# A written-out order of 2440 operations replaced by another: windowed attention and a token-mixing MLP, twice, on one core

## The chip, the cores and the metric

One of the eight cores of a Trainium2 chip runs the whole program. The metric is device time in microseconds, from the first to the last thing that the program does. The engines are PE (TensorE, matmuls; PEld is its weight load), DVE (VectorE), ACT (ScalarE), POOL (GpSimd) and SP (SyncE, which here issues all DMAs, in its own order).

## The reference

The input x has 2048 rows of 512 in bf16. Two layers of two parts each are applied, with the same weights in both layers:

```python
x = x + attention(layernorm(x), wqkv, wo)            # 32 heads of 16, row i sees rows i-255..i
x = x + mlp(layernorm(x), w1, b1, w2, b2)            # mixes the rows, not the columns:
#   h = layernorm(x);  u = gelu(h^T @ w1 + b1)       # 512 x 1792
#   y = (u @ w2 + b2)^T                              # 2048 x 512
```

The attention is `softmax(q k^T / 4 + window mask) v`, then a projection by `wo`. The LayerNorms have no gains, and the MLP's input is normalised twice.

## The kernel before, in words

x stays in SBUF as 16 tiles of 128 rows. Per layer the kernel goes through these steps.

- **LayerNorm** (`ln_blocks`, L499): statistics on DVE (L492, L494), the power -0.5 on POOL (L505), the normalised row tile `xh_sb` on DVE (L512). The two normalisations in a row before the MLP are done as one.
- **Transposed x and projections** (`qkv`, L556): four blocks of 512 rows. `xh_sb` is transposed on PE (L570, copied out at L577 by DVE or L579 by ACT) in the first block, and by DMA elsewhere (L563). PE then projects q, k and v in steps of two matmuls of 128x512 (all of these, and every other dense matmul, go through `mm_group`, L540, and so have line L534). The results leave PSUM by DVE or ACT: q at L592 or L594, k at L603 or L602, or through `stg` (L614) and then a masked copy on POOL or DVE (L629), or eight small DMAs on SP (L624), v at L649 or L651 and from there by DMA into `vb` (L654).
- **Attention** (`attention`, L682): 152 score steps in all, 76 a layer. A score step has 8 to 28 matmuls on quarter-height tiles (L710; L721 adds a mask bias in some steps of the first chunks), writes four of the eight PSUM banks, and is followed by two exponentials on ACT (L736), one for each pair of banks. Where the mask isn't added on PE, POOL multiplies part of the probabilities by zero or one (L757). A P·V step has 32 to 64 small matmuls (L774); two such steps fill two banks, which DVE transposes (L794), inverts (L798), and, after a product on POOL or DVE (L800 or the same line), transposes back into `oT` (L805).
- **Output projection** (`wo_block`, L810): PE by L534, then an addition on DVE (L816), and the LayerNorm for the MLP.
- **MLP**: `u_part` (L869) computes partial sums over the rows that are ready while the attention goes on, and parks them in SBUF (L880, L882, L884); `u_last` (L888, matmuls L895) adds the last rows, DVE adds the parked part (L906), ACT applies gelu (L910). `y_block` (L928) computes y with matmuls by L534 and adds it to x on DVE (L936); in layer 0 the next layer's LayerNorms and projections are mixed in. For the last row tile `y_last` (L914) does the same in two halves of 256 columns (L922). In layer 1 the rows are then written out (L982, halves L925).
- **Weights of the MLP** come tile by tile from HBM, 128 KB a DMA, into four buffers for w1 (`load_w1`, L825), and into two buffers for w2 and, for the first three pairs of row tiles, into free buffers of the probabilities (`load_w2`, L840). A load waits until the last reader of its place is done, and since SP issues in order, everything behind it on SP waits too.

**What sets the order.** None of these functions emits an instruction. Each calls `op` of `Graph` (L107), which records an operation with what it reads and writes; some operations carry alternatives on another engine (`alts`). At the end `Graph.replay` (L175) goes through a list of pairs (which of the operations left, which alternative), takes buffers in that order (`Pool.take`, L63), and appends each operation to its engine's queue; `Graph.emit` (L196) then writes five instruction streams, with semaphore waits for what an operation reads and for the earlier users of its buffers. The list is a constant: `ORDER` (L15), packed text, which `begin_order` (L44) unpacks:

```python
raw = zlib.decompress(base64.b85decode("".join(ORDER)))
left, out = list(range(n)), []
for lo, hi in zip(raw[:n], raw[n:]):
    k, alt = divmod(lo + 256 * hi, 4)
    out.append((left.pop(k), alt))
```

So the order on every engine, the engine of each movable operation, and which buffer a tile gets, are all in that text.

Of the kernel before, what the change touches and what calls it, by code (L numbers as in the profile page):

```python
# [11 lines left out]
P = 128  # L12


ORDER = (  # L15
    'c-p;IA&l$T6@5<LtlqS5E3foc@=E@aw=!@gw{j(~WMJTxyp>ln2uP~{Z)K250RaI90R{mEUMV0TAi%&NARr*XARr(hARr)MfI&b&KvV^!(trU0z0PDZG'
    'yl)uzq{)8{y&cW{N8={o_p?j=Ia9EYe}!&L?lJXYD57>h99@89fUDLp4X6kUl)BtcN|Bvzq7yl24gnw>EBc;?T`h*e!p}DhuPnGE8AYJ>?NDc-EU{JnQ'
    'J?<nJLSPGG|{)lB7yQMUn<-s^rO^wmT_FllgSHMyo7)=X^gB#doRt=XP6FyItG%ZO?`+R26o09>x<(6iusP_r={V77bOCO-)l(#u(3gZN@4UCbX31K~Y'
    'YpHNRo}@kqenZGLz6@UYz)#yfp|x8T?7wXO>bO%SFNVItfMN6Pd2j$$dw=3p3G-2P&<Y=g}gb4}CuEaQ3KR}^J1i1i*=oI^m0jRpykB*?Pc5`=D#Qkrx'
    'kzUzmb(QTUTJuml~KQvpz;jkIhr$Jx`RI0aYLEzVtR?wHE?mso@FZD*F(R5v1g*<O-UX8#F{M2gO?QUDEZE}IE8FM@zHW~>6t5j=MjnGaE0V$RhT9nXk'  # L20
    'w`-V&VR_!x6GdIuD-|+xMbF=7WV>}-*Cn@r1DLLlM&uo(13?r;ScW=0>-0J#jvpv*nNdV1lL^n-`_H#@x7lotBtPCC<2c?Q_J@^ux3R2^Y38Q0PWSu$z'
    'qdPQV4CI%Kmk-I<1r*VG^eu^wlvLdk`B|9F@=f!fgtoDu+K(Gk_2rL3ry+ts4NJOej|)Jov_ge^1N}Uv;sxJg;lFHr&fjfGRrs|7}GSY+~qlyWqG+eMX'
    '_GBbbUHC3@po1Ivz_<?P|5^7p40uf(rnoS&ce#-Fn+zg{EnthG7&Ak?vL;86i#t7qAr|Bgw!|G0P;GW*CDvwgH}sqSWo`Xe{tNY};%$Wu;!1Wr_$91c5'
    '^ga^e|P7|-}@f*2Ht@>SOr1bXm0l*d@6r_%{s7Yhh%O}GtsqPznIpleOwm&<Iym_S*Yf|DxiLEX38eR6|ibT%#(@6t3yBd`=o=ZBP`F1!G*3?qt~jYP4'
    'kgt)RULyJiWqa>-zYnVdn7<s;fTnJdD$Z{(Xu;Chp;~Fl)dZH(TfvsyQa_WYupjy*|*K)0fR8<2`nt?hN5Tu%UIz_`_C5@s%y#uV_J3$Z(0&Lrr3P!}R'
    'N4Bi5okqQ0Z%Fc9SF2k6Un;oJG=-AMVllVAow6MnO#9$&EWQIcTCLWXj5QiRemRN&0^uvxG6QJ2dZR8$;Hb_sCd+8IlPjoNMHQa^f}eho*+5MD*0Kn2D'
    'XCN{EnQb(vg>ve57%lAkN`Wji?L;UI*5j7Xoju;eeey``u-l@Km}w09XEKtPvKS(@Amt}av|YD?;y8ioF>U4fk62VA90;dM^<EwwlG#y#mi29)sN$}dH'
    'he*+v^7K!uK^?m;HbIy&$e6N0JkU4~}CTpyRf?{qA&{O_y0VnqW4}*=D;L4gq16VmzH<oK5X4gG8XkXX8m`nt}kKCgSgI?a_ENf_fq}91V}?2m#~WZim'
    'CLANG0<@TqH>F@P6wb&R=|>tafAvmF#V0|w3INEOM1U(>ejA!q5J6u<$u;sTsVqpEG++YUV(_KxdpWZ>7_vaETnHl02^)E0zz9-7VMnj(X8D@BtSh5@}'
    'F>6YCNLstdYElFUkNl_sEP;`i@_`YgX6jfr9^ZnoQd@{+$o2~EP<^CFbfa+{E1zD9mk4=HYUkd(c2r}XU!4t?6_K^52$tF5zDyZ+|gia^e_1)ocjG`z>'  # L30
    '@-*>0j~^sFZ`*ON(+ZFUUV|3QhgxaJqwh0j8?DwFl-jawWLw}K5C(;dpcRp6nU?LGPNs!TKm(ou;;%`8i@rb$&6cFYfldV2)f5R)fQJeYrQh!>P&7$yQ'
    'fm9YEAoOMY9Jx%{lh&JY6x6SQzHG5tgrw~fD>e%g<&|If~=0m(ReWIC(zj_jan@TEog%Vn=Qzlv_nEL4`9Yl6k1iw4PD0p7usKmsu!kqI!#hQBQ=V`aw'
    '2rd351J*zA*HF5Y$&Y96_fw4GxjbMpemru~v*_R9%1+wkD>!P}TV?QI&452OB3TA&^lIw88HXo)rCvJx6n#*wV1)_dQiL;3QIUo@0cmD9gH%0W*2F90?'
    '*C7AFb_5n*w3x{XQ5aYqQ$q9Bh56l&;zkfY*>5|ZacV6_mVX58=jy(NlKG>GEy#0G(Kp=X0ut5&UsehZ^EvVtaRG#i#v#kK?TRkbX>@M@TrYT1#BR7nM'
    ';!$ejrCPD*?Vl3)uYViW9uT}z#RCPG}RZjw486rN<^*e#bD@aA4bdG1D7>0PYI2^M5@^BbGOeQllo{WQ>F<SH$%kSZM1ZsqFFP_LyKY*&Af&kN0KJ*PE'
    '3?u3{+x~n$M`(!`i{_+g<~oKZu2wQQj0TM~brQoik!iG>aLBs`)Z8!tHIo`xLb5DM5IOp}_W4_bpMCV<**K1a3;JcoT^4ZXmE742hsx#i*bP_wme1oi*'
    'DcOtW$wBYei|yQ7$}u~YR4k_#|bwVub+sp1paPbq<HiAP`dmPL`wJ^#nS{*y2QYt3nb^fN>_03`IGlL|7vCQ_CvY+VOZt2f#hCzyxv^~xtAl5RjIfXae'
    'd4ni4uCl?N1e%d)}GDPa}^oaKDrs*Erq+;NvlWlmMkSAbX1L0?{*tAL-0}!0>B^k4w%Fa$Na?$*;QN?cU%%3gB;SfB1FFKEHC0!j-;+mA;1g{Qvi;^aA'
    'qIxhlow=KXp+*6XowuR!F^tl?gh_z6?YJyzj58*{H||Ev#>-B~W*UfSt(qurt><tP{b&bKgj_EWwLl;3YjRQ?GHmP({_&bNf#7Nk<?b?#4~6_?VJc3ep'
    'IDSaxwC(n9v{;=e(gZMQH_!*D#HJh7q!CiC#;L`&Bh{Xr(SjKOO#``JbYduOY^DmWN-EgIgdOX#={HYU!<31Frw+F5*{6fusMISs<@}&>%g@#-;g?s<~'  # L40
    'OMQHNd>npS#c|KeUZ(aUo&TXiaL>W~Tn+jtA%8<PdrLX5U|tT`r%#AiHF@vn=LPuxP~iUpKz>0O'
)

def begin_order(n):  # L44
# [971 lines left out]
```

## Time and profile before

| | |
|---|---|
| runs before | 446.86, 447.12 and 448.62 us, median 447.12 |
| profiled execution, span from first to last instruction | 443.6 us |
| what lies around the span | 3.3 to 5.0 us, by these runs (the profiled execution's own total is not listed apart) |
| PE busy | 426.4 us, 96%, 6344 matmuls |
| ACT busy | 317.4 us, 72% |
| DVE busy | 308.7 us, 70% |
| POOL busy | 207.9 us, 47% |
| granted TensorE clock | 1.00 throughout |
| DMA | 45.01 MB, mean 101 GB/s |

The profile is of one execution. Its lines name engine, source line, tiles and shapes; a line of a helper (L534) stands for many uses, told apart by their tiles. A "step" below is one recorded operation, for instance two matmuls of a projection. The stages in time: projections of the first blocks and first scores until some 57 us, attention of layer 0 with projections and partial MLP sums between until 151 us, the first MLP and the next layer's first projections until 215 us, attention of layer 1 until 360 us, the last MLP until the end.

### The profile page before, as it was taken

To read this page: it belongs to the slowest core of one execution; us is meant where nothing else is said; L and a number is where in the kernel's file an instruction comes from. 1 tells how busy PE (TensorE), PEld (TensorE's weight loads), DVE (VectorE), ACT (ScalarE), POOL (GpSimd) and SP (SyncE) were. 2 spreads that over 40 slices of the span, in tenths; PEclk is the share of its full clock that TensorE was granted. 3 is DMA by queue.
4 is the path that set the end of the run, shared out by engine and by line. 5 is a ranking of instruction groups with operands and counts; after the bars stand their busy time and mean duration, and the time that the engine had idled before them with its cause. 6 is when DMAs were issued, how large, how long until landed. Compare 5 with 4: busy or idle time off the path is not lost.

```text
span 443.6 us, 14593 instructions
## 1 busy us (share of the span) xinstructions
PE 426.4 (96%) x6344; PEld 193.6 (44%) x6344; DVE 308.7 (70%) x573; ACT 317.4 (72%) x362; POOL 207.9 (47%) x316
## 2 busy tenths in 40 slices
PE   7898989999999999999999999999999999999996
PEld 6453444444433444444444444443344444444452
DVE  7997778778896579564787777789988456521134
ACT  3998999999999941726989899999999870440000
POOL 3486445746486531011566687968867751000000
PEclk9999999999999999999999999999999999999999
DMA  8574522301143446632255322131130447763533
GB/s 244 161 127 73 105 66 47 84 16 30 46 106 92 133 117 185 183 89 71 63 100 154 89 40 57 45 94 23 34 93 15 111 125 197 210 182 102 149 94 106
DMA packets 98736, 45.01 MB, mean 101 GB/s; under 512 B 28912, under 2 KB 98672, under 8 KB 98672
## 3 DMA queue, kind: packets, MB, share of 16 engines
q1 hardware_dynamic: 98672, 44.07, 39.1%
q8 instruction: 50, 0.82, 0.8%
q14 instruction: 14, 0.11, 0.1%
HBM read 33.56 MB, written 2.10 MB: 80 GB/s over the span
## 4 chain that ended last, share of the span: by engine, by line
PE 80%; ACT 12%; DVE 6%; issue 1%; POOL 0%; POOLq 0%
PE PS L534 54%; ACT pt L736 12%; PE PS L710 9%; PE PS L895 8%; PE PS L774 8%; DVE kbd L603 1%; DVE stats L492 1%; DVE xh_sb L512 1%; PE PS L721 1%; DVE rl L794 1%; DVE bb L472 0%; DVE qT L592 0%; DVE stg L614 0%; PE PS L570 0%; DVE vst L649 0%
## 5 line engine op out<-in xcount | busy, mean ns | idle before, releaser
L736 ACT ACTIVATE pt<-PS 128x1024 bf16<-128x1024 f32 (+1 forms) x304 | 281.7, 1036 | 16.0 <-PE PS L710 12.2
L757 POOL TENSOR_TENSOR pt<-pt,ldm 128x256 int32<-128x256 int32 (+2 forms) x226 | 145.1, 668 | 81.6 <-ACT pt L736 79.1
L534 PE MATMUL PS<-xh_sb,w1b 128*128 128x512 bf16 x280 | 68.9, 381 | 0.4 <-ACT pt L736 0.2
L534 PE MATMUL PS<-uT,w2b 128*128 128x512 bf16 (+1 forms) x294 | 69.1, 369 | 0.0
L534 PE MATMUL PS<-xhT,wqkv 128*128 128x512 bf16 (+1 forms) x288 | 67.0, 357 | 2.0 <-issue 0.6
L710 PE MATMUL PS<-qT,kbd 32*128 32x256 bf16 (+4 forms) x1488 | 60.2, 251 | 4.3 <-ACT pt L736 2.1
L505 POOL TENSOR_TENSOR rstd<-agg,mhalf 128x2 f32<-128x2 f32 (+1 forms) x33 | 22.8, 693 | 73.3 <-DVE agg L494 73.3
L936 DVE SCALAR_TENSOR_TENSOR x_sb<-PS,b2col,x_sb 128x512 bf16<-128x512 f32 x31 | 22.9, 746 | 46.6 <-PE PS L534 46.5
L794 DVE STREAM_TRANSPOSE rl<-PS 128x1024 f32<-128x1024 f32 x32 | 39.7, 1242 | 13.8 <-PE PS L774 13.3
L710 PEld LDWEIGHTS PS<-qT,kbd 32*128 32x128 bf16 x1488 | 21.6, 92 | 62.5 <-ACT pt L736 43.4
L910 ACT ACTIVATE uT<-rl,b1col 128x512 bf16<-128x512 f32 x28 | 18.5, 713 | 40.1 <-DVE rl L906 40.1
L774 PE MATMUL PS<-pt,vb 64*17 64x320 bf16 (+4 forms) x2976 | 43.5, 252 | 3.8 <-issue 1.9
L492 DVE BATCH_NORM_STATS2 stats<-x_sb 128x6 f32<-128x512 bf16 x64 | 43.1, 682 | 1.0
L534 PE MATMUL PS<-uT,pt 128*128 128x512 bf16 x168 | 41.2, 379 | 0.0
L534 PEld LDWEIGHTS PS<-uT,w2b 128*128 128x128 bf16 x294 | 27.2, 98 | 31.2 <-issue 3.2
L774 PEld LDWEIGHTS PS<-pt,vb 64*17 64x17 bf16 x2976 | 31.2, 84 | 19.1 <-issue 9.2
L534 PEld LDWEIGHTS PS<-xh_sb,w1b 128*128 128x128 bf16 x280 | 23.7, 98 | 31.8 <-issue 6.2
L895 PE MATMUL PS<-xh_sb,w1b 128*128 128x512 bf16 x168 | 37.4, 379 | 0.0
L534 PEld LDWEIGHTS PS<-xhT,wqkv 128*128 128x128 bf16 x288 | 23.9, 97 | 28.9 <-issue 5.5
L534 PE MATMUL PS<-wqkv,xhT 128*128 128x512 bf16 x128 | 33.9, 381 | 0.5 <-ACT pt L736 0.3
L534 PE MATMUL PS<-wo_sb,oT 128*128 128x512 bf16 x128 | 32.5, 380 | 0.2 <-DVE oT L805 0.2
L512 DVE TENSOR_SCALAR xh_sb<-x_sb,agg,rstd 128x512 bf16<-128x512 bf16 x64 | 29.7, 484 | 2.7 <-POOL rstd L505 2.5
(64 smaller groups left out, 339.8 us busy)
## 6 DMA issues: line engine op xcount, KB each, us to landing
w1b<-in_B_w_dram SPq DMA_DIRECT2D x112, 128.0 KB, 2.8
w2b<-in_B_w_dram SPq DMA_DIRECT2D x70, 128.0 KB, 2.8
pt<-in_B_w_dram SPq DMA_DIRECT2D x42, 128.0 KB, 2.8
vb<-vst SPq DMA_DIRECT2D x64, 68.0 KB, 2.1
out_dram<-x_sb SPq DMA_DIRECT2D x15, 128.0 KB, 2.0
x_sb<-in_A_x_dram SPq DMA_DIRECT2D x3, 512.0 KB, 7.5
wqkv<-in_A_wqkv_dram SPq DMA_DIRECT2D x4, 256.0 KB, 3.8
kbd<-stg SPq DMA_DIRECT2D x48, 16.0 KB, 1.9
```

The source lines that it names most:

```text
L492: op("vector:stat", lambda e: e.bn_stats(st[:, 0:6], x_sb[:, t, :]), reads=[f"x{t}"], writes=[("st", i)], cost=dve_cost(512))
L505: op("gpsimd:rstd", lambda e: e.tensor_tensor(rstd[:, t0:t1, 0], agg[:, t0:t1, 1], mhalf[:, 0:1].to_broadcast([P, t1 - t0]), op=ALU.pow), ...
L512: op("vector:xh", lambda e: e.tensor_scalar(xh_sb[:, t, :], x_sb[:, t, :], agg[:, t, 0:1], rstd[:, t, :], op0=ALU.subtract, op1=ALU.mult), ...
L534: return e.matmul(o, lhsT=w, rhs=x, start=start, stop=stop, skip_group_check=True)
L710: last = e.matmul(bank(tt[r // 2], r % 2)[:, base + c0 * 64:base + (c0 + n) * 64], lhsT=kbd[32 * r:32 * r + 32, tk.slot, o, jj].rearrange( ...
L736: op("scalar:exp", lambda e, ts=ts, tp=tp, i=i, cols=cols: e.activation(probs(tp)[:, i, 0:cols, :], pair(ts)[:, :, 0:cols].rearrange("p r ...
L757: return e.tensor_tensor(v, v, m, op=ALU.mult)
L774: last = e.matmul(bank(t, h)[32 * r:32 * r + 17, i + q0 * 64:i + (q0 + n) * 64], lhsT=vb[64 * h:64 * h + 64, tk.slot, jj, 4 * o + r, :], r ...
L794: op("vector:od", lambda e, t=tod, tr=tr: e.transpose(rl[:, tr.slot:tr.slot + 2].rearrange("p a b -> p (a b)"), pair(t)), reads=[(tod, i) ...
L895: last = e.matmul(bank(tu, tt), lhsT=v()[:, sc - b0, k0 + tt * P:k0 + (tt + 1) * P], rhs=xh_sb[:, sc, :], start=(sc == b0), stop=(sc == NT ...
L910: op("scalar:gelu", lambda e, ft=ft, tt=tt: e.activation(uT[:, ft, :], rl[:, tmps[tt].slot], ACTF.Gelu_apprx_tanh, bias=b1col[:, ft:ft + 1 ...
L936: op("vector:resy", lambda e: e.scalar_tensor_tensor(x_sb[:, t, :], bank(ft), b2col[:, t:t + 1], x_sb[:, t, :], op0=ALU.add, op1=ALU.add), ...
```

## The change

The 27 lines of packed text in `ORDER` are replaced by others. Nothing else differs.

```diff
 ORDER = (
-    'c-p;IA&l$T6@5<LtlqS5E3foc@=E@aw=!@gw{j(~WMJTxyp>ln2uP~{Z)K250RaI90R{mEUMV0TAi%&NARr*XARr(hARr)MfI&b&KvV^!(trU0z0PDZG'
...
+    'c-qZYJ&5br6~3~s-`;t97xcni&;u=~(87H|3n~=Q1{Eq4&<iRYaG}D50}5zCg$f5$s8B!w7b={ffC>j(xNzaZg$oxh9B|>ng$ox`xNzaZg$oz2n8JiykH<5f'
...
```

Unpacked, both lists hold the same 2440 operations. The number of operations on each engine, and of those that change the engine:

| engine | before | after |
|---|---|---|
| PE | 922 | 922 |
| DVE | 559 | 552 |
| ACT | 359 | 369 |
| POOL | 299 | 294 |
| SP | 301 | 303 |

46 operations change the engine, among them six products from POOL to DVE and four back, five q copies from DVE to ACT and three back, four parked sums from DVE to ACT, three first-block k copies from DVE to ACT and one back, two v copies from DVE to ACT, and eleven masked k copies among POOL, DVE and SP (eight on SP after, six before).

The places that the prediction speaks of, as the two lists have them. The matmul steps around the first two pairs of P·V steps (score, projection with its output, P·V):

```
before: score  q-proj q-proj  score  q-proj k-proj k-proj  score  PV PV  score
after:  score  q-proj q-proj k-proj  score  k-proj  PV  score  q-proj  PV  score

before: score  q-proj q-proj q-proj  score  q-proj  PV PV  score
after:  score  v-proj q-proj  PV  score  q-proj q-proj  PV  score
```

DVE at the start (each name one instruction; `sel`, `bb`, `par`, `half` prepare masks):

```
before: ... bb stat(row tile 1) eps sel agg(1) stat(0) agg(0) half xh(1) sel par sel bb xh(0) bb xhT ones ldm stat(3) stat(2) ...
after:  ... bb stat(1) par agg(1) stat(0) par agg(0) bb bb half half xh(1) xh(0) stat(2) xhT ldm stat(3) ldm ldm sel q ...
```

SP at the start: x tiles 2 and 3 are loaded third instead of fifth; x tiles 12 to 15 come after the first transposing DMAs instead of before them; some w1 loads change places. DVE before the output projection of chunk 3: a row of L512 that stood directly ahead of a transpose of L805 stands further up. At the end of PE the last group of the program is a half of `y_last` instead of a whole `y_block`. In the last MLP the weight loads stand in another order on SP, among themselves and against the rows that are written out.

More of the change, by code (lines that the diff above doesn't have):

```diff
@@ new lines @@
+    ')`$JxH1Bq+jk&WZ71wKhHIp^D;Z0^!B-dr&3gD1;v+kZWqo%5=>vel$nj{r1Yq`)DG0}wSWH?aOuZM$f924KC)uNzzpW1J`-36UnU7<S>1mm^N`$;Qn`K{S3'
+    'ihOYwMR61=VbM&}UyV|}ANBmCD@SoVmm>yJ!1KQE2aZ!U?7;K=;}L|%FvN5(iqU4CWt;fl_3gUGyMiIkz8Bnjqt25;XE{3UTvbU^a6-dKlEnS9N_5=<Q4}<>'
+    ';d!dAy8urn-r*oCk~}c%Thp>7Q?gzQgb=l-^b|!QLZ{tM#k438NnqR}N5ZG+hzygP-DcN8>kYcS-S6METE=3#O}B=zT;8rsbA7v5E~j*{+Zk))_IA}VO~Y8U'
+    'TFb?7HXP1oGsl6tJ~H2ShL*(-x`V-RkjuQT5C4*}?_Q#HjIN&U_pTVnO{tybLbG{ycSq9{vOigdq9-<M3=y9-jCZgjI;LcZ`a2zNt5CITP+2TYWeR6A)0|93'
@@ new lines @@
+    'HpQ|$kO#lU7#FTPbK$;~wKGL=p`BC9wpyv`iZBv1IaDDbhN@|>fvED5ic*EG5U)aXI0%SRijbm=$75X)ByoWH{VtV>po@Ac2#l4A+9WVgD9`h<C^Q_Av3o~#'
+    'T{m87ia;n41wjx+jW2kJu__8GAp!Kk5nz0XBgt_<A0a^&5F(q+hFc?M1QY(<yMA9FJSx~6-4-z4Z4km{E6Y?wXKX5Yv;}|z{XFmHdE#eT27t~+MwKHlhta?l'
+    'SrBMNJU{@5%uGWXuK<Jq17f)dIfxn<hpie=Y|yMX!%zZLX~?oADAblD$U=$Y@VrS4p0N7fQH5%%#@MDRbT;dG6P`dBSf(i{GqHv=YTNa?>Jo&J>$-N$wnN*K'
+    'n7K6>RyRPz)(H&FK@jlxWH8UAZwCYPO`Ktr;w<~y&COp~o!I6nzVS`XKw_hzDE^Ir2ol{I>&4B6(f)v`B`g+rPH^=rhs}4t-#2^H)YbJ`H4H;H2!d#5J4k_X'
@@ L42 @@
+    ')S)L>&$zz)^2_t;<wqHLy8GpW7oOfapU+I0@v;0UFlY6+Ka@YOch902n=bTvl#0@|z?7cXe0p&{UAbIhXBAfN7pJqz7atR$7hhDkk5B?$fpfa{SmeF*z;np`'
+    'g-bkqD*jyUnQ-M#R{B&WEI&%}b7A@*@~P0PHGE$4mH3{ZI-ym1u#fTSaXc?y<xe%|GMG==_c*59WqJYk{;tFQM7?=WF}Y{b_57*l)^HrhanJI)R*{FZN6~&r'
+    '@qy;tl^ij_zE|zbF7spb^5FsHpL3(<e)5aKFKFBc`^p9KN8o;mSDl~3{saH+IMM'
 )
```

39 lines of the change are left out of this document (14 added, 25 removed).

## Prediction

> **What bounds the kernel now.** I read the page first (PE busy 426.4 of 443.6 us), then the stages, because an average over stages with different limits says little. The columns are: stretch, its length, and the busy time of PE, PEld, DVE, ACT and POOL with the instruction counts, clock, DMA share and GB/s.
>
> ```profile
> 10.20:57.00 46.80, 41.81 (x1015) 22.43 (x1023) 39.90 (x88) 43.18 (x51) 27.32 (x36) 1.00 0.59 124
> 57.00:127.20 70.20, 65.90 (x1445) 29.37 (x1435) 56.75 (x98) 68.68 (x74) 39.33 (x60) 1.00 0.21 47
> 150.60:214.80 64.20, 64.20 (x470) 28.26 (x466) 42.67 (x76) 30.96 (x41) 10.32 (x16) 1.00 0.44 122
> 214.80:343.80 129.00, 128.19 (x2235) 53.55 (x2238) 105.68 (x182) 121.51 (x133) 95.64 (x145) 1.00 0.30 69
> 343.80:443.60 99.80, 96.14 (x703) 44.34 (x702) 39.87 (x69) 27.15 (x34) 15.63 (x23) 1.00 0.50 142
> ```
>
> From 150.6 us on PE is the bound and hardly idle: only a change of its work or a late load can count there. From 57 to 127 us ACT is busy 98%: the exponentials of L736 set the pace, and PE's idle time is a consequence. From 10 to 57 us no engine is full, so this is where order can pay; whatever ACT wins there moves the full stretch behind it. The timeline of ACT shows where it stood (start, length, operation; in brackets the idle time and its releaser):
>
> ```profile
> 22.34 13.14 ACT L736 ACTIVATE pt<-PS 128x1024 bf16<-128x1024 f32 x14 [0.20 <-PE PS L721]
> 37.22 9.27 ACT L736 ACTIVATE pt<-PS 128x1024 bf16<-128x1024 f32 x10 [1.74 <-PE PS L710]
> 47.55 9.27 ACT L736 ACTIVATE pt<-PS 128x1024 bf16<-128x1024 f32 x10 [1.05 <-PE PS L721]
> 57.01 3.77 ACT L736 ACTIVATE pt<-PS 128x1024 bf16<-128x1024 f32 x4 [0.18 <-PE PS L721]
> ```
>
> Ten exponentials take 9.27 us, so one follows another in 0.91 us. The two long holes wait for scores (L710, L721). The chain of waits says why those were late:
>
> ```profile
> 33.67 1.20 PE PS L774 x90
> 34.87 1.39 issue
> 36.26 0.57 PE PS L774 x25
> ...
> 44.78 1.37 PE PS L774 x103
> 46.15 0.54 issue
> 46.68 0.30 PE PS L774 x8
> ```
>
> Both times two P·V steps (L774, 64 matmuls each) run back to back, and in the second one PE stops for nothing that a semaphore shows. The page has a queue of kind "instruction" whose row gives 50 packets and 0.82 MB, some 16 KB each. In the trace two of its packets begin at 33.24 and 43.69 us, and the stops end at 36.26 and 46.68, 3.0 us later in both cases. My reading: the P·V steps used up their instructions sooner than the next block came.
>
> **The change, part by part.** Every matmul, exponential and load stays: 6344 matmuls in both programs, 304 exponentials. Only orders and 46 choices of engine differ.
>
> *Matmul work.* A two-matmul projection step takes 0.43 us in a run of its kind and 0.53 ahead of a step with another tile shape (rows of L534: 0.54 for x2, 1.40 for x6). Such places number 146 before and 149 after. With all steps priced by their neighbours the sum is 419.3 us before and 418.8 after; from the last quarter of layer 0 on, where PE is the bound, both have 285.4. I take 0, bounds -0.5 to +0.5.
>
> *Start.* Before, the second LayerNorm row starts at 7.00 us although POOL delivered its rstd at 6.51, since four short mask preparations stand ahead of it:
>
> ```profile
> 6.20 0.18 DVE L465 COPY sel<-ident 32x128 bf16<-32x128 bf16 x1
> ...
> 7.00 0.41 DVE L512 TENSOR_SCALAR xh_sb<-x_sb,agg,rstd 128x512 bf16<-128x512 bf16 x1
> ...
> 7.90 0.42 DVE L577 COPY xhT<-PS 128x512 bf16<-128x512 bf16 x1 [0.37 <-PE PS L570]
> ```
>
> After, four such stand ahead of the first row: it starts near 6.2 (5.88 before), the second near 6.5, then one statistic of 0.6, and the copy of L577 at 7.45, 0.45 earlier. The third x load is issued two places sooner, which that statistic needs. One q copy goes from ACT, where it followed a 0.86 pair, to DVE: another 0.25. So the first exponential comes 0.7 earlier. DVE is the tight engine here, and its 1.2 us transpose of L794 at 29.46 stands behind one more statistic; walked on by the same rows, the scores at 30.96 come only 0.25 earlier. I take -0.3, bounds -0.9 to +0.5.
>
> *First pair of P·V steps.* After, a score step and a projection step (0.53) stand between the two. The two P·V steps take 0.62 and 0.82 us without the stop (128 matmuls in 1.45), a score step of this form 0.41. From the end of the score step between them to the end of the next one PE now has 0.53 + 0.82 + 0.41 = 1.76 us and the stop, against two exponentials of 1.81. The stop itself: if the fetch still begins at the same instruction of the stream, PE has 1.8 to 2.25 us of work instead of 1.63 until it runs dry, so 0.75 to 1.2 us of stop. ACT's hole becomes about 1.76 + 1.0 - 1.81 - 0.15 of backlog = 0.8 instead of 1.9: -1.1, bounds -1.9 and -0.3.
>
> *Second pair.* After, a score step and two projection steps stand between. From score to score: 0.43 + 0.53 + 0.82 + 0.41 + 0.36 of stop = 2.55 against 1.81, less some backlog; the stretch before it grows by 0.4. The hole is about 0.75 instead of 1.28: -0.5, bounds -1.2 and 0.
>
> By the row the stops are a fetch that PE outruns. The Trainium skill, "Runtime: NRT & Kernel Launch", Instruction fetch mechanics, says that instructions come in 16 KiB blocks of 256 through a queue of the sequencer's own, and that crossing a block is mostly hidden. The packet size agrees with the 16 KB of the row, the "hidden" does not: 1.39 and 0.54 us of PE are at stake. By the rule taken strictly the stops would be something else, and spacing would not shorten them; that is the first rival.
>
> *One normalisation less ahead of the last output transpose of chunk 3.* DVE at 124.08 runs a row of L512 (0.86 on the chain) before L805 (124.94), for which PE waits; after, that row is gone from there. PE's wait there is 0.2 to 0.5: -0.3, bounds -0.5 and 0.
>
> *Engine moves.* ACT gets ten more evacuations (0.47 us each in a run), in layer 1's first 16 score steps mainly and before the last MLP, where ACT has 121.5 of 129 us and 27 of 100: hidden by PE, cost 0; if not hidden, +1. Two more block-diagonal K writes go to SP (L624), eight DMAs each, about 3.7 us of SP; at least 3.7 us of matmuls stand between them and their reader: 0.
>
> *The end.* The last group is now 256 wide instead of 512: its add takes 0.48 instead of 0.75 (L922 against L936), and the output row behind it is 64 KB. -0.3, bounds -0.6 and 0.
>
> *Loads in the PE-bound part.* This speaks against the change. I counted, for each weight load, the matmul time between its turn at SP (after what frees its place) and its first reader.
>
> ```profile
> w1b<-in_B_w_dram SPq DMA_DIRECT2D x112, 128.0 KB, 2.8
> w2b<-in_B_w_dram SPq DMA_DIRECT2D x70, 128.0 KB, 2.8
> ```
>
> Before, the least is 3.8 us in the last 90 us of the kernel; after, four places have 2.54, 2.75, 2.81 and 2.95 (a w1 load of the last MLP, and three w2 loads, one of them for the last two groups). At the median landing of 2.8 that is 0.26 + 0.05 late, 0.3 in all; at 3.06, the median of the 56 loads issued from 370 us on, 0.52 + 0.31 + 0.25 + 0.11 = 1.2; at 3.55, the slowest of these, 3.15. I take +0.4, near the first, since much of that queue is waiting loads that the new order issues at other times; bounds 0 and 3.2.
>
> Sum: -0.3 - 1.1 - 0.5 - 0.3 - 0.3 + 0.4 = -2.1 us, so a span of 441.5 for 443.6. The runs shown (446.86 to 448.62) lie 3.3 to 5.0 above the span, their median 3.5; taking 2.1 from the median 447.12 gives **445.0 us**.
>
> **The rivals.**
> 1. *Given back.* The stops are no matter of spacing, and ACT's hole moves to the next scores. For: the score steps themselves keep their count of exponentials, and the full ACT stretch is as long as before. Against: the 3.0 us seen twice. Only the start and the end remain, -0.6, and the loads, +0.4: 446.9 us.
> 2. *Slower: late loads.* The four thin places above find landings of 3.55 us, 3.15 us late in all, and the gains up front fail as in the first rival. For: DMA is busier in the last 100 us (share 0.50) than in the mean, and PE has no idle time there to hide in. Against: the median of 2.8. 447.12 - 0.6 + 3.15 = 449.7. It decides from landings of about 3.5 us.
> 3. *More.* Both holes go altogether (-1.9 and -1.2), the start keeps its 0.7, the rest as above and nothing is late: 447.12 - 4.4 = 442.7.
>
> That the order changes nothing at all is excluded by the listing of the programs: 1670 lines of difference on PE alone.
>
> **How the numbers follow.** Forecast 0.55, from 443.7 to 446.5 by its own bounds; given back 0.19; late loads 0.11; more 0.15. About 0.5%, 2.2 us, is what a measurement of this kernel can tell from no change: the border is 444.9. Of the forecast's 0.55 a half lies under it, so faster 0.27 + 0.15 = 0.42, same 0.28 + 0.19 = 0.47, slower 0.11. The range reaches to the third rival and nearly to the second: 442.0 to 449.0.
>
> **What would show it.** Right: the holes of ACT near 36 and 46 us at 0.8 and 0.7 or less, the "issue" pieces inside L774 shorter, the first exponential near 10.1, ACT 98% busy until some 125 us, and the start of the first MLP's dense stretch 2 us earlier. The loads: PE idle before L895 near 382 us and before L534 near 390, 426 and 436 us, with a load as releaser, 0.3 to 1.2 us in all. Wrong: "issue" stops of the old length or at new places, DVE (L794, L603) as releaser of PE through the first 30 us, or PE idle by microseconds behind 360 us.

## The result, and the profile after

The changed kernel takes 458.33 us (median of 4 runs, 457.69 to 458.91) against 446.99 (4 runs, 445.92 to 448.62): ratio 1.0256, 95% interval 1.0231 to 1.0282. It is 11.3 us slower, and 9.3 us above the upper end of the range. The profiled execution took 458.22 us with a span of 456.5; the span before was 443.6, so 12.9 us are to be found. The granted clock is 1.00 in both.

The busy time of the engines per stretch, for the same five stretches (start:end, length, busy us and instructions of PE, PEld, DVE, ACT and POOL, clock, DMA share, GB/s):

```profile
10.20:57.00 46.80, 36.18 (x866) 19.41 (x864) 39.38 (x81) 37.94 (x45) 21.98 (x28) 1.00 0.47 100
57.00:127.20 70.20, 63.65 (x1402) 28.27 (x1400) 57.62 (x102) 66.45 (x73) 33.82 (x52) 1.00 0.28 54
150.60:214.80 64.20, 62.89 (x549) 28.15 (x542) 40.47 (x73) 31.98 (x41) 15.68 (x23) 1.00 0.44 124
214.80:343.80 129.00, 127.12 (x2084) 52.83 (x2089) 96.06 (x165) 122.78 (x141) 92.46 (x136) 1.00 0.33 75
343.80:456.50 112.70, 107.39 (x937) 48.65 (x914) 47.23 (x80) 39.70 (x50) 22.32 (x33) 1.00 0.45 130
```

In the first stretch, where the gain was expected, PE gets through 866 matmuls where it did 1015, and is busy 5.6 us less; ACT is 5.2 us less busy. The second loses 2.2 us of both. In the last three, PE was idle for 0, 0.8 and 3.7 us; now it is for 1.3, 1.9 and 5.3. The chain that ended last, by engine, has two new names, and its second line says which transfers:

```profile
PE 68%; ACT 9%; DVE 8%; SPq 6%; DMA 6%; issue 2%; POOL 0%; POOLq 0%
PE PS L534 47%; ACT pt L736 8%; PE PS L710 8%; PE PS L895 7%; PE PS L774 6%; DMA w1b<-in_B_w_dram 4%; SPq L624 2%; DVE xh_sb L512 2%; SPq L654 2%; SPq L830 1%; DVE stats L492 1%; DMA vb<-vst 1%; DMA kbd<-stg 1%; DVE qT L592 1%; SPq L563 1%
```

Before, it was PE 80%, ACT 12%, DVE 6%. Now 12% of the span is SP's queue and DMA: w1 loads, masked K writes (L624), V blocks (L654). The timeline of ACT, with the holes in brackets:

```profile
9.87 6.58 ACT L736 ACTIVATE pt<-PS 128x1024 bf16<-128x1024 f32 x8 [0.79 <-PE PS L710]
19.50 0.59 ACT L651 CAST vst<-PS 128x512 bf16<-128x512 f32 x1 [3.05 <-PE PS L534]
...
36.57 3.90 ACT L736 ACTIVATE pt<-PS 128x1024 bf16<-128x1024 f32 x4 [1.91 <-PE PS L721]
42.35 7.44 ACT L736 ACTIVATE pt<-PS 128x1024 bf16<-128x1024 f32 x8 [1.89 <-PE PS L710]
50.05 1.94 ACT L736 ACTIVATE pt<-PS 128x1024 bf16<-128x1024 f32 x2 [0.26 <-PE PS L710]
52.76 7.44 ACT L736 ACTIVATE pt<-PS 128x1024 bf16<-128x1024 f32 x8 [0.76 <-PE PS L721]
```

The first exponential comes at 9.87, even earlier than forecast. The hole of the first P·V pair is as long as before (1.89 at 42; 1.74 in the kernel before), another of 1.91 stands ahead of it, and the longest, 3.05, comes right behind the first exponentials.

**Where the 12.9 us went.** I followed each score step by its number, counted from 0; both lists have the score steps in the same sequence. Its delay against the kernel before is -0.8 us for the first, +2.1 for number 4, +5.1 for number 12, +8.5 for number 44 (95 us in the kernel before), 8.1 for number 72 (151 us, first layer), 10.0 for number 80 (215 us, second layer), 11.5 at 352 us and 12.9 at the end. Then I took each step of PE that started later than the usual spacing from its forerunner allows, and looked for what it waited for:

| at us | PE late by | it waited for |
|---|---|---|
| 13.8 | 3.2 | a K evacuation on DVE (L603), late behind two long DVE rows |
| 32.1 | 2.0 | the last of four DMA transposes (L563), 4.3 us from issue to landing |
| 39.1 | 2.0 | nothing a semaphore shows, in the second P·V step (before: 1.65) |
| 67.0 | 1.0 | a masked K write that had moved to SP (L624) |
| 98.8 | 1.4 | V blocks (L654), ready at 80.0, issued by SP at 94.2 |
| 179.1, 344.6, 375.5, 394.9 | 1.3, 0.6, 0.4, 1.2 | w1 loads (L830) |
| 328.4, 330.9 | 0.7, 0.5 | two normalisations (L512) |

With 0.3 for the third row they sum to 12.6; the 0.8 gained at the start and smaller gains and losses are not in the table. It is of one execution: in the traces of experiments 4 and 16 below, which follow the changed order to 215 and 128 us, number 4 is 4.6 and 3.5 us late where it is 2.1 here, and number 12 is 9.1 and 5.7 late where it is 5.1. The first row is the largest, and had not been in my sum: PE stands 3.15 us ahead of L534 at 17.38, with DVE's L603 as the releaser. The chain of waits there, and the timeline of POOL beside it:

```profile
12.07 1.43 DVE sel L465
...
14.22 2.32 DVE xh_sb L512 x2
16.54 0.79 DVE kbd L603 x2
...
17.38 0.61 PE PS L534 x4
```

```profile
11.65 1.80 POOL L482 MEMSET kbd<- 128x2048 f32 x1
...
14.45 1.95 POOL L482 MEMSET kbd<- 128x2048 f32 x1
```

The copy into `sel` takes 0.18 us everywhere else. Here it begins at 12.07, beside a memset on POOL, and ends at 13.50; the memset ends at 13.45. The second of the two L512 rows takes 1.97 instead of 0.41 and ends at 16.54; the second memset ends at 16.40. The kernel before runs these memsets at 24.50 to 28.15.

The third row of the table is the stop that the prediction wanted to shorten:

```profile
39.17 0.42 PE PS L774 x34
39.59 1.80 issue
41.39 0.57 PE PS L774 x24
```

It stands behind the 36th matmul of the second P·V step, before behind the 37th: the same place of PE's instruction stream, number 1217 of its listing in both. It ends 1.46 us after a packet of the queue "instruction" has ended, which now runs from 38.99 to 39.93 (before: 33.24 to 34.88, and 1.39). The stop of the second pair has shrunk to 0.18 us, at 51.79 (before: 0.54).

The masked K write of the fourth row, in the chain of waits:

```profile
65.29 3.22 DMA kbd<-stg
68.51 0.05 issue
68.56 0.42 PE PS L710 x8
```

Eight small DMAs keep SP from 59.4 to 65.9, and the last lands at 68.51: 9.1 us for a copy that POOL did in 1.36. In the loads' own rows, w1 has its 2.8 as before, w2 takes 2.6 (before 2.8), and the w2 tiles in buffers of the probabilities 3.3 (before 2.8):

```profile
w1b<-in_B_w_dram SPq DMA_DIRECT2D x112, 128.0 KB, 2.8
w2b<-in_B_w_dram SPq DMA_DIRECT2D x70, 128.0 KB, 2.6
pt<-in_B_w_dram SPq DMA_DIRECT2D x42, 128.0 KB, 3.3
```

These are medians. The four w1 loads that PE waits for in the table were issued at 177.04, 342.68, 372.27 and 392.98 and landed 3.7, 2.8, 4.5 and 3.5 us later. So they come late by SP's order, by their landing, or by both; no run tells the two apart.

### The profile page after: what moved, and what is told of

Its sections match the earlier page's. It is cut to its first block, busy times and chain, and to the rows that moved or that the text cites. A ratio compares the mean times of both kernels' runs of the same rounds, so it can differ in the third digit from the quotient of the medians.

```text
span 456.5 us, 14601 instructions
## 1 busy us (share of the span) xinstructions
PE 428.0 (94%) x6344; PEld 193.4 (42%) x6344; DVE 308.0 (67%) x566; ACT 324.7 (71%) x374; POOL 205.2 (45%) x307
## 4 chain that ended last, share of the span: by engine, by line
PE 68%; ACT 9%; DVE 8%; SPq 6%; DMA 6%; issue 2%; POOL 0%; POOLq 0%
PE PS L534 47%; ACT pt L736 8%; PE PS L710 8%; PE PS L895 7%; PE PS L774 6%; DMA w1b<-in_B_w_dram 4%; SPq L624 2%; DVE xh_sb L512 2%; SPq L654 2%; SPq L830 1%; DVE stats L492 1%; DMA vb<-vst 1%; DMA kbd<-stg 1%; DVE qT L592 1%; SPq L563 1%
## 5 line engine op out<-in xcount | busy, mean ns | idle before, releaser
L757 POOL TENSOR_TENSOR pt<-pt,ldm 128x256 int32<-128x256 int32 (+2 forms) x226 | 147.7, 679 | 95.4 <-ACT pt L736 94.1
L534 PE MATMUL PS<-xhT,wqkv 128*128 128x512 bf16 (+1 forms) x288 | 68.5, 357 | 7.5 <-DVE kbd L603 3.1
L534 PE MATMUL PS<-xh_sb,w1b 128*128 128x512 bf16 x280 | 69.9, 381 | 2.0 <-DVE xh_sb L512 0.9
L534 PE MATMUL PS<-uT,w2b 128*128 128x512 bf16 (+1 forms) x294 | 69.0, 370 | 0.0
L534 PE MATMUL PS<-uT,pt 128*128 128x512 bf16 x168 | 41.2, 379 | 0.0
L895 PE MATMUL PS<-xh_sb,w1b 128*128 128x512 bf16 x168 | 37.9, 379 | 2.4 <-DMA w1b<-in_B_w_dram 2.4
L534 PEld LDWEIGHTS PS<-uT,w2b 128*128 128x128 bf16 x294 | 27.1, 98 | 30.7 <-issue 3.5
L534 PEld LDWEIGHTS PS<-xhT,wqkv 128*128 128x128 bf16 x288 | 23.9, 97 | 33.9 <-issue 6.4
L534 PEld LDWEIGHTS PS<-xh_sb,w1b 128*128 128x128 bf16 x280 | 23.6, 97 | 34.3 <-issue 6.3
L512 DVE TENSOR_SCALAR xh_sb<-x_sb,agg,rstd 128x512 bf16<-128x512 bf16 x64 | 33.7, 550 | 3.3 <-POOL rstd L505 3.1
L534 PE MATMUL PS<-wqkv,xhT 128*128 128x512 bf16 x128 | 34.7, 381 | 0.0
L534 PE MATMUL PS<-wo_sb,oT 128*128 128x512 bf16 x128 | 33.3, 380 | 0.0
```

The lines of the kernel that those rows point to most:

```text
L512: op("vector:xh", lambda e: e.tensor_scalar(xh_sb[:, t, :], x_sb[:, t, :], agg[:, t, 0:1], rstd[:, t, :], op0=ALU.subtract, op1=ALU.mult), ...
L534: return e.matmul(o, lhsT=w, rhs=x, start=start, stop=stop, skip_group_check=True)
L757: return e.tensor_tensor(v, v, m, op=ALU.mult)
L895: last = e.matmul(bank(tu, tt), lhsT=v()[:, sc - b0, k0 + tt * P:k0 + (tt + 1) * P], rhs=xh_sb[:, sc, :], start=(sc == b0), stop=(sc == NT ...
```

## The experiments

All but the hybrids are the list of one kernel with a few entries moved. `behind(i, j)` takes operation number i (numbers as recorded) out of the list and puts it right behind number j. A hybrid follows one list to a given operation and then all that is left in the sequence of the other. Added lines shift the line numbers of these kernels: L512 is L517 in the first, L519 in the ninth.

**1 and 2. The memsets, undone and alone.**

```diff
+    behind(47, 156)   # changed order: the memsets behind the masks, as before
+    behind(48, 47)
```
```diff
+    behind(47, 92)    # order of before: the memsets early
+    behind(48, 125)
```

> The changed order, with one thing undone: the two memsets of kbd on POOL (L482, 1.80 and 1.95 us in the changed kernel's trace, at 11.65 and 14.45) go back to where the kernel before has them, behind the masks for the score steps. Theory A (POOL holds DVE up: a DVE copy or normalization from SBUF to SBUF that starts beside a long POOL operation ends only with it; the copy into sel took 1.43 us instead of 0.18 and the second xh row 1.97 instead of 0.41, and the first K evacuation behind them came so late that PE stood 3.2 us at 13.8): both rows are short again, the stall at 13.8 is gone, and the kernel gains 2 to 3.2 us of its 458.3, so 455 to 456.3. Rival B (the two rows are long for a reason of their own, or the 3.2 us are waited out at the next transposes anyway): 457.8 to 458.8, with the scores from number 12 on as late as in the changed kernel.

> The order of before, with one part of the change alone: the two memsets of kbd on POOL (L482) moved ahead, one right behind the third rs row, one behind the first mask operation, about where the changed order has them (12 to 16 us). Theory A (POOL holds DVE up): DVE rows L465, L472 or L512 that fall beside a memset grow from 0.2 to 0.4 us to as much as 2, PE gets its first K and q steps later, and the kernel loses 1.5 to 3.2 us of 447.0: 448.5 to 450.2. Rival B (POOL's place is free): 446.5 to 447.5.

Measured: 457.83 (ratio to before 1.025, 1.0213 to 1.0288), no gain; and 446.61 (1.0002, 0.9986 to 1.0018), no loss. By the times rival B. The trace of experiment 1 says otherwise. Three rows of it, of DVE, of POOL and of PE:

```profile
22.74 4.54 DVE L517 TENSOR_SCALAR xh_sb<-x_sb,agg,rstd 128x512 bf16<-128x512 bf16 x3
```
```profile
22.72 3.69 POOL L487 MEMSET kbd<- 128x2048 f32 x2
```
```profile
28.58 0.41 PE L715 MATMUL PS<-qT,kbd 32*128 32x64 bf16 x24 [3.81 <-DVE rl L799]
```

Score number 4 was 2.8 us earlier, as theory A has it. But the memsets now ran beside three normalisations, of which two took 1.92 and 1.97 us and ended 0.14 us behind a memset each; what DVE had next came late, and PE stood 3.8 us there. In the second experiment DVE was idle and then had an evacuation from PSUM beside the first memset, and statistics beside the second, of usual length; no normalisation met a memset, so it could not show theory A. In the kernel before they stand beside evacuations and statistics too. So the place of a memset on POOL is free, or costs PE 3 us there, by what DVE does at that moment.

**3 and 4. The halves.** The cut is at 215 us, at the fifth score step of the second attention (the expectations call it the first).

```diff
+    head = first[:[i for i, _ in first].index(1198) + 1]
+    done = {i for i, _ in head}
+    return head + [x for x in then if x[0] not in done]
```

> The order of before up to the first score step of the second attention (some 215 us), then all that is left in the changed order, with the changed engines. In the traces the changed kernel's score steps lag by 9.7 to 10.0 us there and its end by 12.9. Theory A (each loss is made where it shows, and the second half's is made by its own order): 2 to 3.5 us above before, 449 to 450.5. Rival B (the second half only pays for the first half's lateness, in late loads and rows): within 1 us of before, 446.5 to 448.

> The other half: the changed order up to the first score step of the second attention, then all that is left in the order of before. Theory A (losses are made where they show): 9 to 10.5 us above before, 456 to 457.5. Rival B (the lateness of the first half is what costs the second half too): 458 to 459, as the changed kernel. If the first half's loss is partly made up behind the cut: below 455.

Measured: 451.33 (1.0103, 1.008 to 1.0126) and 456.70 (1.0231, 1.0184 to 1.0278), 4.9 and 10.3 above the runs of before beside them. Theory A, with the second half 0.8 us dearer than its range, and a sum above the whole.

**5 to 8. Three repairs of the changed order.** 5: the memsets where DVE has no normalisation. 6: six transfers earlier on SP. 7: all 46 engine choices as before. 8: all three.

```diff
+    behind(47, 125); behind(48, 47)                         # 5
+    behind(503, 177); behind(429, 500); behind(975, 976)    # 6
+    behind(1930, 1862); behind(2145, 2133); behind(2160, 2159)
+    out = [(i, alts.get(i, a)) for i, a in out]             # 7
```

> The changed order, its two memsets of kbd (L482) on POOL moved a second way: behind the first six mask operations, where VectorE has evacuations from PSUM and statistics for some 4 us (16.5 to 20.5 in the trace of the first try), and no normalization of a token tile. Theory A, as the first try left it (POOL's memset holds VectorE up only where VectorE reads and writes SBUF alone: in the first try two rows of L512 took 1.92 and 1.97 us beside the moved memsets and ended with them, and PE stood 3.9 us at 24.2 instead of 3.2 at 13.8): neither stall, no VectorE row of 1.9 us before 30 us, score number 4 about 2.8 us earlier than in the changed kernel and numbers 8 and 12 by 2 to 3; of that 1.5 to 3 us are left at the end, 455.3 to 456.8. Rival B (whatever is won here is waited out at the next transposes and at the instruction packets near 40): score number 16 as late as in the changed kernel, 457.5 to 458.5.

> The changed order, its engines and its matmul order as they are; six transfers are moved up in SP's order and nothing else: the copy of V blocks for PE's stall at 98.8 (vb), the four w1 loads for the stalls at 179.1, 344.6, 375.5 and 394.9, and one early w1 load put behind a transpose instead of ahead of it (stall at 32.1). Theory A (PE stands there because SP issues the late one behind less urgent ones: 1.39 + 1.27 + 0.62 + 0.38 + 1.22 us, and about 0.6 of the 2.01 at 32.1): these stalls go or shrink to under 0.4 each, 4 to 5.5 us less than the changed kernel, 452.8 to 454.3. Rival B (slots and the transfers' own rate set the landing, so another load is late in its place): less than 1.5 us gained, 457 to 458.5.

> The changed order with all 46 engine choices of before put back (masked K writes from SP to POOL and VectorE, evacuations between VectorE and ScalarE), the order of all 2440 operations as changed. Theory A (of the engine choices only the masked K write on SP costs PE time: it landed 9.1 us after its issue, and PE stood 1.0 us at 67.0): 1 us gained, 456.8 to 457.8. Rival B (order and engines were found together, and the old engines in the new order collide): slower than the changed kernel by 1 us or more, above 459.

> The changed order with all three at once: memsets in the third place, the six transfers moved up, the engines of before. Theory A (the causes are separate places on PE's path and add up): 7 to 9 us less than the changed kernel, 449.5 to 451.5. Rival B (a gain at one place is waited out at the next, above all in the first 100 us): less than 5 us gained, above 453.5.

Measured, 5: 456.51 (1.0226, 1.0194 to 1.0259), 1.8 us under the changed kernel, as theory A gave it. POOL and DVE in its trace:

```profile
18.28 3.67 POOL L487 MEMSET kbd<- 128x2048 f32 x2
```
```profile
18.29 1.24 DVE L497 BATCH_NORM_STATS2 stats<-x_sb 128x6 f32<-128x512 bf16 x2
19.45 0.31 DVE L499 BATCH_NORM_AGGREGATE agg<-stats 128x2 f32<-128x9 f32 x2
19.68 1.62 DVE L608 TENSOR_SCALAR kbd<-PS,par 128x256 bf16<-128x256 f32 x4
```

Statistics of 0.62 and K evacuations of 0.41 us beside the same memsets: nothing is held up. Score number 4 is 2.8 us earlier than in the changed kernel, number 12 by 2.0, the later ones by 1.5 to 2.4. So the first row of the table is worth about 2 us of the 11, by the trace. The times alone don't show it: the four runs, 456.25 to 458.67, overlap those of the changed kernel, 457.69 to 458.91.

Measured, 6: 458.41 (1.0261, 1.0228 to 1.0295), no gain: rival B by the time. Four of the five stalls named were gone, the fifth, at 375, grew (PE idle 0.90 us where it was 0.21), and the transpose's was 1.48 instead of 2.01. The chain shows two places where it was given back. The stop in the second P·V step grew, since PE reached it 0.55 earlier and the packet came no sooner (39.38):

```profile
38.62 0.43 PE PS L783 x34
39.05 2.71 issue
41.76 0.57 PE PS L783 x26
```

and in the last stretch, where SP issues a load every 0.51 us within a group, a w1 load and a w2 load were late:

```profile
370.67 4.28 DMA w1b<-in_B_w_dram
...
400.71 3.53 DMA w2b<-in_B_w_dram
```

In the first half 1.3 us were held (score steps at 215 us late by 8.7 instead of 10.0).

Measured, 7 and 8: 478.17 (1.0693, 1.0656 to 1.0731) and 475.14 (1.0637, 1.06 to 1.0674), 20 and 17 us above the changed kernel. Rival B of the seventh, far beyond its bound. Two other masked K writes are on SP in the choice of before, and in the changed list their turn comes late. SP's own timeline has the first behind a transposing DMA:

```profile
85.78 1.21 SPq L565 DMA_TRANSPOSE xhT<-xh_sb  x1
87.04 5.99 SPq L626 DMA_DIRECT2D kbd<-stg  x8
```

They were issued at 87.0 and 101.6, though their inputs were ready at 61.7 and 70.1, and PE stood 4.5 and 3.0 us for them and 2.0 for V blocks behind them. In this list an operation's engine and its turn belong together, and the engines can't be undone alone, so experiment 8 tells nothing of adding up.

**9 to 11. The prediction's gains alone, in the order of before.** 9: four projections between the P·V steps of the first pair. 10: the changed order up to its second score step. 11: both.

```diff
+    behind(190, 253); behind(191, 190); behind(194, 191); behind(195, 194)   # 9, 11
+    head = first[:[i for i, _ in first].index(127) + 1]                     # 10, 11
```

> The order of before, with term two of the prediction's sum done alone and more strongly: four projection steps (1.75 us of PE by their own spacing) moved between the two P.V steps of the first pair, from right behind them. In both traces so far PE's stop stands at the same place of the program, at the 35th or 36th matmul of the second P.V step, and its end comes 3.0 us behind a packet of the queue named instruction, which started at 33.24 in before and only at 38.99 in the changed kernel. Theory A (the packet starts by its own, at some 33.2, and work put ahead of the stop fills it): the stop shrinks from 1.64 us to under 0.3, the four projections are done beside it, 1.0 to 1.7 us are won on PE and 0.5 to 1.5 at the end, 445.3 to 446.5 where before gives 446.8. Theory B (the packet starts when PE comes within some way of the place, so spacing moves it along, as the changed kernel's trace suggests): the packet starts 1 to 2 us later, the stop stays over 1 us, and the time is that of before within 0.5 us.

> Term one alone: the changed order (and engines) up to its second score step, 11 us, then all that is left in the order of before. Theory A (the earlier start is real: first score step 0.8 us earlier in the changed kernel, and what came after it was lost to the memsets on POOL, which stand in the place of before here): first score step 0.6 to 0.9 earlier, and 0.3 to 0.8 of it kept to the end, 446.0 to 446.5 where before gives 446.8. Rival B (the mask preparations that were put off come due between 11 and 18 us, as the prediction's upper bound has it): the fourth score step no earlier or up to 0.5 us later than in before, 446.6 to 447.5.

> Both of the last two in the order of before: the changed start up to the second score step, and the four projections between the first pair of P.V steps. If both theories A hold and add up: 1 to 2.2 us less than before, 444.6 to 445.8. If only one of them does: 445.5 to 446.5. If neither: 446.5 to 447.5.

Measured, 9: 447.16 (1.0025, 1.0005 to 1.0045), slightly slower. PE and ACT:

```profile
36.54 0.84 PE L781 MATMUL PS<-pt,vb 64*17 64x64 bf16 x64
37.31 0.41 PE L717 MATMUL PS<-qT,kbd 32*128 32x64 bf16 x24
38.85 0.40 PE L717 MATMUL PS<-qT,kbd 32*128 32x256 bf16 x8 [1.13 <-ACT pt L743]
```
```profile
37.77 5.76 ACT L743 ACTIVATE pt<-PS 128x1024 bf16<-128x1024 f32 x6 [2.02 <-PE PS L717]
```

The first half of theory A holds: the packet starts at 33.47, 3.2 us ahead of its place, and the second P·V step runs its 64 matmuls in 0.84 us without a stop. The second half falls: the score step behind comes at 37.31 (before 36.76), ACT's hole is 2.02 (before 1.74 on its row, 1.9 in all), and the next score step then waits for ACT with no projection left to do meanwhile.

10: 445.63 (0.9988, 0.9971 to 1.0005): 1.1 us by the medians, not told apart from before. In its profile the first score step is 0.8 us earlier, number 4 by 0.2, and number 20 is 0.4 later. 11: 446.66 (1.0006, 0.9987 to 1.0026), no gain, the case of neither theory.

**12. The end alone.** The order of before, from 345 us on the changed one (cut at 2061).

> The end alone: the order of before up to a step at 345 us, then the changed order for all that is left (the last groups of the mixer's first matmul, 256 wide instead of before's arrangement, and the second). The prediction gave this part -0.3 for the shorter last group and +0.4 for late weight loads. Theory A (SP issues a load every 0.51 us from 362 to 400, each group's loads start only when the group before gives its slots back, and the changed arrangement leaves them less time: in the trace of before-then-after these steps lost 0.5 at 368 and 1.0 at 388): 1.5 to 2.5 us above before, 448.3 to 449.3. Rival B (the lateness there came from the earlier part of the second half): within 0.6 us of before.

Measured: 448.98 (1.0064, 1.0038 to 1.0089), 2.3 above before: theory A by the time. PE waits for w1 loads there, which it never did before in that stretch, but also longer for ACT (4.0 us in its row, 1.9 before), mostly right behind the place where the two lists meet:

```profile
PEld PS L746 <- ACT pt L772: 4.0, 6, 1.2
PEld PS L931 <- DMA w1b<-in_B_w_dram: 1.3, 2, 0.8
PEld PS L570 <- DMA w1b<-in_B_w_dram: 0.9, 1, 0.9
```

How much of the 2.3 is the loads' was not measured apart.

**13 to 16. What was still open.** 13: a score step between the P·V steps of both pairs, in the order of before. 14: the same with the changed start. 15: the changed order for the second attention alone. 16: for the first attention alone.

```diff
+    behind(190, 253); behind(191, 190); behind(264, 191); behind(303, 269)   # 13, 14
```

> The order of before with a score step between the two P.V steps of both pairs: in the first, two V projections and the score step that stood behind the pair, in the second the score step alone. Theory A (PE's stop costs only through ScalarE: with the next scores ahead of it, ScalarE has work over the stop): ScalarE's holes of 1.9 us at 35 and 1.28 us at 46 shrink to under 0.8 and 0.7, the packet of instructions still starts near 33.2, and 0.8 to 1.6 us are won, 445.1 to 445.9 where before gives 446.7. Rival B (PE is the bound there as well, or the work that waits for the second P.V step comes late in its turn): the time of before within 0.5 us. Rival C (the score step between moves the packet along, as in the changed kernel): the packet starts over 1 us later, holes as before, and 446.5 to 447.5.

> The changed order up to its second score step (11 us), then the order of before with a score step between both pairs. Theory A: the start alone gave 445.6 against 446.7, and with the score steps 0.8 to 1.6 more, 444.0 to 445.0, the fastest of all. Rival B (the score steps bring nothing): 445.2 to 446.2. Rival C (the starts do not add to a region that ScalarE bounds): 446 to 447.

> The order of before but for the second attention: the changed order and engines stand from 215 us to a score step at some 334 us, and before's order again for the rest. Before-then-after from 215 us cost 4.9 us and the last group alone 2.3. Theory A (the second attention makes its own loss: late V blocks at 295, 1.27, and two normalizations held back behind POOL at 321 and 324, 0.69 and 0.52): 2 to 3 us above before, 448.7 to 449.7. Rival B (the late rows there are covered, and what was left of the 4.9 was the joint with the last group): within 1 us of before.

> The changed order for the first attention alone, up to a P.V step at 128 us of its trace, and the order of before from there on. Theory A (the loss of the first half is made by the attention's order in the first 100 us: the normalizations held up by POOL, the late transposes, the masked K write and the V blocks on SP): 7.5 to 9 us above before, 454.2 to 455.7, as the score steps lag by 7.9 at that place. Rival B (the first mixer's loads share it, with their 2.1 us between 206 and 215, because the lateness reaches them): 456 to 457.5, as with the changed order up to 215 us (456.7).

Measured, 13: 448.24 (1.0027, 1.0005 to 1.005), 1.6 us above before by the medians: slower than any of the three had it, by rival B's mechanism in the trace. 14: 447.46 (1.0015, 0.9994 to 1.0036), no gain, and nearest to rival C. ACT in 13, and PE's next wait:

```profile
36.66 1.94 ACT L743 ACTIVATE pt<-PS 128x1024 bf16<-128x1024 f32 x2 [0.52 <-PE PS L717]
39.35 1.94 ACT L743 ACTIVATE pt<-PS 128x1024 bf16<-128x1024 f32 x2 [0.75 <-PE PS L728]
41.77 5.61 ACT L743 ACTIVATE pt<-PS 128x1024 bf16<-128x1024 f32 x6 [0.48 <-PE PS L728]
47.63 1.94 ACT L743 ACTIVATE pt<-PS 128x1024 bf16<-128x1024 f32 x2 [0.25 <-PE PS L728]
```
```profile
38.82 0.40 PE L717 MATMUL PS<-qT,kbd 32*128 32x256 bf16 x8 [1.44 <-DVE rl L801]
```

The hole went from 1.74 on its row (1.9 in all) to 0.52 as forecast, and came back as 0.75 and 0.48 behind: the next score step waits for DVE's transpose out of the P·V banks (L801), which is later now. The second pair's hole did go (1.05 on its row before, 0.25 now), and neither is seen in the time.

15: 447.87 (1.0021, 1.0001 to 1.0041), 1.2 above before: between the two theories. Its trace shows the three stalls that theory A named (1.45, 0.70 and 0.51). 16: 455.11 (1.0177, 1.0149 to 1.0205), 8.5 above: theory A.

**17 and 18. The complement, and the repairs of the first half.** 17: the order of before up to 145 us, then the changed one (cut at 909). 18: the changed order with the memsets in the third place and three transfers moved up.

```diff
+    behind(47, 125); behind(48, 47); behind(503, 177); behind(429, 500); behind(975, 976)   # 18
```

> The complement of the last experiment: the order of before up to a step at 145 us, where the changed kernel lags by 8, and the changed order and engines for all that is left. Theory A (three quarters of the loss are made in the first attention, and what is made behind it does not hang on the lateness): 447 + 1.6 for the first mixer + 4.9 at most for the second half, less what the sum of the parts passes the whole, so 449.5 to 452.5. Rival B (the later stages of the changed order lose as much whatever comes ahead of them, and the early lateness hides a part of it): above 453.

> The changed order with the memsets in their third place and only the three transfers of the first half moved up (one w1 load behind a transpose at 30, the V blocks at 94, one w1 load at 177); the end is left as it is. Theory A (the repairs add where the end isn't touched: 1.8 from the memsets as measured, 1.3 from the copies as the score steps at 215 showed it): 454.6 to 455.8. Rival B (what one repair gains the stop on the instruction packet near 39 or the next load takes back): 456 to 457.5, no better than with the memsets alone (456.5).

Measured, 17: 449.81 (1.0062, 1.0043 to 1.0081), 2.5 above before: theory A, at its lower end. 18: 455.11 (1.0175, 1.0144 to 1.0207), 3.2 under the changed kernel: theory A. Its trace shows the limit too: the transposes' stall is gone, and the stop in the second P·V step is 3.2 us (2.0 in the changed kernel).

By 16 and 17, about 8.5 to 9 of the 11.3 us are made by the changed order in the first attention, and 2.5 behind it, most of these in the last group (12). The repairs of 18, of which one stands behind the first attention, took back 3.2; the rest is placed by the table and the traces, and no experiment takes it apart. The hybrids' losses sum to more than the whole (16, 15 and 12 alone: 12.0; and 3 costs 4.9 where 17, with more of the changed order, costs 2.5); what the joints add was not measured apart.

No version is faster than the kernel before beyond doubt; 10 comes nearest.

## Why the prediction was wrong

**The start (-0.3) is the step that failed most.** Its first part held: the first exponential came 0.9 earlier (forecast 0.7). But it was "walked on by the same rows" to scores 0.25 earlier at 31 us; they were 5.1 later. The sign of being wrong that the prediction had named, DVE's L603 as the releaser of PE in the first 30 us, came at 17.38 with 3.15 us. Two memsets of POOL, moved from 24.5 and 26.4 to 11.7 and 14.5, had no term at all. And the walk took a DVE row's duration as fixed. The trace of before said that it isn't: the copies into `sel` take 0.18 us and one took 0.70, L512 takes 0.41 and up to 1.23, each ending with the POOL operation beside it. I had read the means. Summed over the kernel, what DVE rows take beyond their group's median rose from some 10 to some 14 us (rows over it by more than 0.05). The traces of experiments 1 and 5 show this cause: the stall goes with the memsets and comes back where they meet normalisations again. In the times, 5 puts it at 1.8 us, within the spread of its runs. The other part of the delay by number 12, the transposes at 32 us (2.0), comes from rows normalised 3 to 6 us later (24.8 to 27.1 where it was 19.3 to 23.8) and four transposes one behind another on SP. That part is read from the trace; 18 removed it together with others.

The Trainium skill, "SBUF — State Buffer", SBUF: two separate sides, says that VectorE and GpSimd share one pair of SBUF ports, that it is an exclusive lock, and that the loser blocks for the whole instruction of the other. The rows agree: 1.97 us for 0.41, ended 0.14 behind the memset. The section Who interferes with whom there excepts VectorE operations with one SBUF input outside the two-port modes; the statistics of 0.62 in experiment 5 agree.

**First pair of P·V steps (-1.1) and second (-0.5).** The reading of the stop as an instruction fetch held for the first pair: in all 16 traces that have the stop at over 1 us, it ends 1.4 to 1.6 us behind the end of the packet, and the work of experiment 9 filled it. The shorter stop of the second pair is tied less closely: in the 13 traces that have it at over 0.4 us, it ends 1.4 to 2.2 us behind its packet. The condition that I wrote with it, "if the fetch still begins at the same instruction of the stream", failed: the packet started 0.9 to 1.4 us ahead of the stop in the order of before, and from 0.4 ahead to 0.7 behind its beginning in the changed one. Why it starts later there is open. And where the stop went (9), ACT's hole stayed, because the next scores came no sooner; where the score step was between (13), the hole returned behind, at the next evacuation by DVE. That is the second half of the first rival, the hole that moves on; its first half, that the stops are no matter of spacing, is refuted by 9. In the changed kernel the first hole stayed at 1.89, so the -1.1 measured nothing. Around the second pair two holes of 0.26 and 0.76 stand where one of 1.05 was, nearly the same in sum, so of the -0.5 little can be seen either.

**Engine moves (0).** A masked K write on SP was priced at 3.7 us of SP, with as much matmul work behind it, and two more of them were reckoned. By the lists fifteen of these writes change their engine (not eleven), and six are new on SP while four leave it. The one shown above keeps SP 6.5 us and lands after 9.1, 1.0 us late at 67 us. The V blocks late at 98.8 (1.4) are no part of this term: SP stood from 77.5 to 83.5 at a transposing DMA that waited for a normalised row, and then had other transfers ahead of them. That is order. Experiment 7 shows what such a write costs when its turn is late.

**Late loads (+0.4, bounds 0 and 3.2).** The mechanism of the second rival, mis-sized: the four w1 stalls of the table sum to 3.5 us, in one place that had been counted (394.9) and three that had not. I had counted the matmul time ahead of each load's reader by its place in the list, and set it against a median landing of 2.8. But SP takes 0.51 us per load, so of two loads that get their place at the same time the second is issued that much later; and three of the four late loads took 3.5 to 4.5 us to land, the landings at which that rival decides. Which of the two weighs more is not shown. The last group alone costs 2.3 (12), of which the loads are a part. The moves of experiment 6 did not mend the last stretch.

**The end (-0.3) and the normalisation at 124 us (-0.3)** are too small to be seen beside this. **Matmul work (0)** held: nothing in the runs calls for a term.

The range failed as a whole because its bounds were put round the gains and the loads, each from the rows it touched. The loss came mostly from what had no term: operations of POOL and SP that changed their turn, and that I had taken as hidden. That it was made in the first attention is shown by 16 and 17; how it divides there is shown for the memsets and, together with them, for three transfers (18), and read from the traces for the rest.

## What to carry to other kernels

Before walking a new order with measured durations, look at the spread within each group of rows: a row of DVE that is three times its median, and ends with an operation of POOL, tells that durations depend on what runs beside them, so an order judged by walking it with fixed durations can be wrong by microseconds. When an order changes, list every operation of the lightly used queues whose turn moved, POOL's memsets and SP's small copies above all, and ask what each now runs beside or stands ahead of. A hole closed ahead of a chain of PE, ACT and DVE can move on to the next of them, as it did in experiment 13.

## What the runs showed of the hardware

- A memset of 128x2048 f32 on POOL (1.80 us) held normalisations on DVE to 1.92 to 1.97 us (0.41 alone) and a copy of 0.18 to 1.43; the wait lies inside the DVE row and shows as no idle time. In the traces of experiments 4 and 16 a normalisation that began beside a short POOL operation ran on through the memset behind it, 2.17 us. Statistics and evacuations from PSUM beside it kept their length.
- PE's instruction stream: between two matmuls at one place of the program, in whichever order, 1.2 to 3.5 us went by, until 1.4 to 1.6 us behind the end of a 16 KB packet. When 1.45 to 1.75 us of other matmuls stood between the two P·V steps in the order of before, nothing was left of it in three traces (9, 11, 13) and 0.46 in one (14). The Trainium skill, "Runtime: NRT & Kernel Launch", Instruction fetch mechanics, calls the crossing of a block mostly hidden; at this place it is not.
- Eight DMAs of 16 KB from SBUF to SBUF kept SP 6.5 us and landed 9.1 us after the first issue, while the page's median from issue to landing of one of them is 1.9.
- The first score step varied by some 1.1 us from profile to profile of one order (9.2 to 10.3 us with the changed start, 10.2 to 11.3 with that of before); what varies there was not looked into.
